# A gated attention-and-MLP kernel: full-array products next to P.V issued as four column strips, memory state as diagonal blocks

## Chip, core and metric

The kernel runs on one core of a Trainium2 chip. The metric is the device time of one execution in microseconds (us). The core's engines run side by side, each through its own list of instructions in order: PE (TensorE, matrix products into PSUM), DVE (VectorE), ACT (ScalarE), POOL (GpSimd) and SP (SyncE, which here only issues DMAs). They wait for one another through semaphores.

## What is computed

One layer over 2048 tokens of width 448, in bf16. A gate per token mixes two branches: attention in four segments of 512 tokens, with a linear memory of the earlier segments, and an MLP that mixes along the tokens.

```python
g = _sigmoid((x * gate_w).sum(-1, keepdims=True))
# attention: H = 16 heads of 28, N = 4 segments of L = 512
for s in range(N):
    p = _softmax(q_s k_s^T * 28**-0.5 + causal mask)
    a_dot = p @ v_s
    num = einsum('bhld,bhde->bhle', phi(q_s), M)
    den = einsum('bhld,bhd->bhl', phi(q_s), z)[..., None] + 1e-06
    o = gh * (num / den) + (1.0 - gh) * a_dot          # gh = sigmoid(beta), per head
    M = M + einsum('bhld,bhle->bhde', phi(k_s), v_s)
    z = z + einsum('bhld->bhd', phi(k_s))
a = o @ wo
# MLP over the token axis, F = 1792
u = gelu(einsum('bsd,sf->bdf', layernorm(x), w1) + b1)
b = einsum('bdf,fs->bds', u, w2) + b2
out = g * a + (1 - g) * b
```

(Indices are shortened; phi(t) is t + 1 above zero and exp(t) below.)

## The kernel before

Everything stays in on-chip memory between input and output. The work is cut into some 600 PE steps with names, and as many on the other engines:

- **Projections** `k0..k3`, `q0..q3`, `v..` (line 679): two products of 64 rows each run side by side on the two halves of the array's rows.
- **Scores** `scP_F` (938): for a pair P of attention units and one of five fills F, four heads at once on four strips of 28 rows. A unit is one segment and one group of four heads; there are 16 units. ACT takes the exponential (947) and POOL sets the masked triangle to zero (950).
- **P.V** `pvU` (975): for unit U, sixteen matmuls, four heads at once on four strips of 32 columns, with moving operands of 512, 384, 256 and 128 columns. The loop over `hl` puts head `hl` into PSUM partitions 32*hl to 32*hl+31. DVE transposes the result (`ta`, 991).
- **Memory** `mstS` (824): after each of three segments, phi(k)^T v as 16 full-array products of 128 by 128, four head groups over four token tiles. All 16 head-to-head blocks of a group are computed. DVE adds them up (`msta`, 837 and 840) and multiplies by `maskg`, which is zero outside the four diagonal blocks (`mstc`, 842). `memU` (961) is one product of 512 columns with that state, and `tm` (989) its transpose on DVE.
- **Output projection** `woT` (1026): four full-array products of 448 columns. `ag` (1032, 1036) takes it out of PSUM on ACT or DVE.
- **MLP** `uF-S` (1046), 14 x 16 products of 448 columns with the full array, and `yT-F` (1075), 16 x 14 of them, the last tile in two parts of 320 and 128 columns. GELU is five steps on ACT and DVE (1050 to 1063), and the output is made on DVE (`fin`, 1080).
- **Transposes of x** for the first 512 tokens, `trx0_0` and `trx0_1` (648): eight of 128 by 128 each, into two banks, then two copies out, `xTcp`, the even one on DVE and the odd one on ACT.

Every PE step has a mode, which the text keeps using: `f` for the full array, `h` for half the rows, `r` for the row strips of scores, `c` for the column strips of P.V.

The order of the steps is written out by hand, as a list of names per engine (`ORDER`); `u0-0:3=6` means the three steps from `u0-0` on, into PSUM bank 6. `Sched.plan` follows these lists and makes each step wait for what it reads and for the step that last used its bank. Banks 4 to 7 are handed round among all these steps; banks 0 to 3 belong to scores after the start. For some steps the list also says which of two engines does them.

Of the kernel before, what the change touches and what calls it, by code (L numbers as in the profile page):

```python
# [5 lines left out]
ACT = mybir.ActivationFunctionType  # L6
ALU = mybir.AluOpType
# [23 lines left out]
NFILL = 6  # L31

# [11 lines left out]
class Op:  # L44
    __slots__ = ("eng", "evspace", "fn", "deps", "order", "is_event", "ev_val", "knowledge", "waits", "name", "idx",
                 "cost", "lat", "prio", "mode", "start", "end", "pos", "nbytes", "alts", "rel", "port", "take",
                 "free")
# [26 lines left out]
class Sched:  # L74
# [13 lines left out]
    def op(self, eng, fn, reads=(), writes=(), name=None, dma=False, out=False, cost=100.0, prio=0.0, mode=None,  # L88
           nbytes=0, rel=0.0, port=False, take=None, use=(), alt=None):
# [14 lines left out]
        o.free = use  # L104
        for g in use:
            g.left += 1
# [45 lines left out]
    def plan(self, order):  # L152
# [7 lines left out]
        for e, text in order.items():  # L160
            seq[e] = []
            for tok in text.split():
                tok, _, banks = tok.partition("=")
                name, _, run = tok.partition(":")
                if run:
                    base, _, k = name.partition("-")
                    got = [byname["%s-%d" % (base, int(k) + i)] for i in range(int(run))]
                else:
                    got = [byname[name]]
                for o in got:  # L170
                    o.eng = e
                for g, b in zip(got[0].take, banks):
                    g.bank = int(b)
                seq[e] += got
        assert sum(len(v) for v in seq.values()) == len(self.ops)
# [28 lines left out]
        self.ops = line  # L204

# [48 lines left out]

def pe_cost(*cols):
    return sum(max(c, 64) / 2.4 + 2.0 for c in cols)
# [10 lines left out]
def pool_cost(n):  # L267
# [7 lines left out]
        warm fill0 fill1 fill2 fill3 fill4 trx0_0=45 fill5 gtr trx0_1=67 v03s v03a v03b v03c v03d k0a=45 k0b=67 k0c  # L275
        k0d q0a q0b q0d q0c v67a=46 sc0_0 k1a=57 v67c k1c sc0_1 k1b=64 k1d sc0_2 q1a=75 q1b=64 sc0_3 q1c q1d pv0=7
        sc0_4 u2-0:2=6 u1-0=5 u2-2:2 u0-0:3=4 u1-1 u2-4 u1-2:3 sc1_0 u2-5 u0-3 u1-5 u0-4 btr=7 u0-5 u1-6 u2-6 u0-6
        u2-7 u0-7:2 u1-7 u0-9 u4-0=7 u1-8:2 u0-10 sc1_1 u0-11 u1-10:3 u2-8:2 u1-13:3 u0-12 u2-10:2 u0-13 u2-12 u0-14
        u2-13 u0-15 u4-1 u2-14 u3-0=5 sc1_2 u4-2 u3-1:2 u4-3 u3-3 u4-4 u3-4 u2-15 pv1=4 sc1_3 u4-5 u3-5:2 u5-0:2=4
        u3-7 u5-2:2 u4-6:2 u5-4 u3-8 sc1_4 u4-8 u3-9 u5-5 u3-10:2 u4-9 u5-6 u3-12 u4-10 u3-13 u5-7 u3-14:2 u5-8:2  # L280
        u6-0=6 u4-11 u5-10 u4-12 sc2_0 u4-13 u5-11:2 u7-0=5 u4-14 u6-1 u7-1 u4-15 u7-2 u5-13 u6-2 u7-3 u6-3 u5-14
        sc2_1 u7-4:2 mst0=7 u7-6 u5-15 u7-7:3 u6-4:2 u7-10 sc2_2 pv3=7 pv2=4 u6-6:2 u8-0:3=7 u6-8:2 u7-11 u6-10 sc2_3
        u8-3 u7-12 u6-11 u7-13:3 u6-12:2 u9-0:2=4 u8-4 u6-14:2 u8-5 sc2_4 u8-6 u9-2 u8-7:2 u9-3 u8-9 u9-4 mem4=5
        u9-5:3 sc3_0 u8-10 u9-8 u8-11:2 u9-9:3 u8-13:3 u9-12:4 pv4=6 sc3_1 k2a=57 k2b=46 k2c k2d sc3_2 q2a=75 q2b=46
        q2c q2d sc3_3 v96a=57 v96b=46 v96c v96d sc3_4 pv6=7 pv5=5 u10-0:4=4 u11-0=6 u10-4 mem5=7 u10-5 mem6=5 u10-6
        u11-1 sc4_0 u13-0=7 u10-7 u13-1:2 u10-8:6 u11-2:3 sc4_1 u10-14 u13-3 u11-5 u13-4 u10-15 u11-6 u12-0=5 u11-7
        u12-1 u11-8 u13-5 u11-9:3 u12-2 u11-12:2 u13-6 sc4_2 u12-3:2 u11-14 u13-7 u12-5 mst1=4 u13-8 u11-15 u13-9
        u12-6 sc4_3 u12-7 u13-10 u12-8:2 u13-11:2 mem7=6 u12-10 u13-13 wo1=4 u12-11 sc4_4 pv7=6 wo0~2=4 u12-12
        u13-14:2 u12-13:3 wo3=6 wo2=4 sc5_0 k3a=67 k3b=54 k3c k3d sc5_1 v14a=67 pv8=5 v14c sc5_2 pv9=5 wo5=4 mem9=6
        q3a=75 q3b=46 q3c q3d sc5_3 mem8=5 y1-0:3=7 y0-0=4 y1-3 y3-0=6 y1-4:2 y0-1:2 y1-6 y0-3:2 y3-1 y1-7 y3-2:3 y1-8  # L290
        sc5_4 y1-9 y3-5 y0-5:2 y1-10 y0-7 wo4=5 y1-11 sc6_0 y0-8:2 y3-6 y0-10:2 y3-7 y1-12 y0-12:2 y3-8 y1-13 sc6_1
        y3-9:2 y4-0:2=5 y3-11 y4-2:2 y3-12 y4-4 y3-13 mem11=7 wo6=4 sc6_2 y4-5 mst2=7 pv11=6 pv10=4 sc6_3 y4-6 mem10=7
        y2-0=6 y4-7:2 y2-1 y6-0=4 y4-9 y2-2 y6-1 y4-10 sc6_4 y5-0=7 y6-2 y2-3:2 y4-11 y5-1 y2-5 y5-2 y6-3 y5-3 y6-4
        sc7_0 y2-6:2 y5-4 y4-12 y2-8 y5-5 y2-9 y5-6 y6-5 y4-13 y2-10 y5-7 sc7_1 y2-11 y5-8:2 y6-6 y2-12 mem12=5 y2-13
        y5-10 y6-7 y5-11:2 sc7_2 y6-8:4 y5-13 wo7=6 pv12=5 sc7_3 y6-12 mem13=7 y7-0:3=6 wo8=5 y7-3 y6-13 wo10=7 y7-4
        pv13=5 sc7_4 y7-5 wo9=4 y7-6:2 y8-0=7 y7-8 y9-0:2=5 y7-9:2 y9-2 mem14=4 y7-11 y8-1 y7-12 y9-3 y8-2 y9-4 y8-3:2
        y7-13 wo11=4 y8-5 y9-5 pv15=6 pv14=4 y9-6 y8-6 y9-7 mem15=6 y8-7:2 y9-8 y10-0=4 y9-9 y8-9:2 y10-1 y8-11 y9-10
        y10-2:2 y9-11 y11-0=6 y10-4:2 y11-1 y8-12 y10-6 y9-12 y11-2 y9-13 y8-13 y10-7:2 y11-3:7 y10-9 y11-10 y10-10
        y11-11 y10-11 y11-12 y10-12:2 y11-13 wo12=5 wo13=7 wo14=6 wo15=4 y12-0=5 y13-0:2=7 y12-1 y15-0=6 y12-2 y15-1
        y14-0:2=4 y13-2:2 y14-2 y13-4 y14-3 y12-3 y15-2 y14-4 y15-3 y13-5 y14-5:2 y13-6 y14-7 y12-4 y15-4 y13-7 y12-5  # L300
        y13-8 y14-8 y15-5 y14-9 y13-9:2 y15-6 y14-10 y15-7:2 y14-11 y13-11 y14-12 y15-9:2 y13-12 y15-11 y13-13
        y15-12:2 y12-6:2 y14-13 y12-8:6 y15-0~2=7 y15-1~2 y15-2~2 y15-3~2 y15-4~2 y15-5~2 y15-6~2 y15-7~2 y15-8~2
        y15-9~2 y15-10~2 y15-11~2 y15-12~2 y15-13~2
    """,
    "ACT": """
        ldx1 ldgwb ldgw xTcp0_01 xTcp0_11 cpv2 cpv0 cpv3 gt1 gt0 cpk0_0 gt3 gt2 ek0_0 cpk0_2 cpk0_3 cpk0_1 cpq0_3
        cpq0_2 cpq0_1 gt4 ek0_1 exp0_0=2 cpv6 gt7 gt6 exp0_1=3 cpk1_2 exp0_2=4 exp0_3=0 cpq1_2 tb cpv5 gt5 exp0_4=1
        ek0_2 eq1_1 exp1_0=5 exp1_1=6 gsq1 eq1_0 eq1_2 gsq0 exp1_2=2 ek0_3 gth0 exp1_3=3 gsq2 gth1 exp1_4=0 gth2 gsq3
        ek1_0 ek1_1 exp2_0=1 gsq4 gth3 exp2_1=4 gsq5 gth4 gvh5 eq1_3 exp2_2=0 gth5 ek1_3 exp2_3=3 gsq7 gsq6 exp2_4=2
        gth7 gth6 exp3_0=5 gsq8 gsq9 gvh9 ek1_2 exp3_1=6 cpk2_1 cpk2_3 cpq2_3 exp3_2=1 cpq2_1 cpv8 gt8 exp3_3=4 cpv10  # L310
        gt10 gt9 ek2_0 eq2_1 gt11 gt12 exp3_4=7 ek2_1 gth9 gth8 exp4_0=5 exp4_1=6 eq2_0 gsq10 gvh10 exp4_2=0 gsq11
        gvh11 exp4_3=2 gth10 ag1 gth11 exp4_4=3 gsq13 gsq12 gvh13 gvh12 ek2_2 exp5_0=1 cpk3_0 exp5_1=4 cpq3_3 cpv14
        cpv15 gt14 gt15 gth13 gth12 ag5 exp5_2=7 ek2_3 cpq3_0 cpq3_2 gt13 eq3_1 exp5_3=5 eq2_3 eq3_0 eq2_2 exp5_4=6
        exp6_0=0 exp6_1=2 ag6 exp6_2=3 eq3_2 exp6_3=5 exp6_4=6 exp7_0=1 exp7_1=4 exp7_2=7 ag7 exp7_3=0 ag8 ag10 ag9
        exp7_4=2 eq3_3 ag11 ag12 ag15
    """,
    "DVE": """
        bns0 bna0 bns1 xTcp0_00 gw bns2 xTcp0_10 padk0 bns3 bna1 padq0 bna3 padq2 bna2 cpv1 padq3 ln0 ln2 ob0 mk0_0
        phk0_0 gcol0 ln3 bns4 cpv4 cpq0_0 bns5 bns7 bna4 bns6 bns9 bna5 cpv7 mk0_1 cpk1_1 ln1 bns13 cpk1_0 bna6 cpk1_3
        bna7 cpq1_3 bna13 bns8 bns11 bns15 bna9 bns10 cpq1_0 bna10 bna11 ln6 bna8 cpq1_1 bna15 bns14 ln4 ln9 bns12 ln5  # L320
        ln7 bna14 omgh ta0 ln8 gh ln10 bna12 oc0 b1c mo0 ln11 b2c oc1 ln13 mk0_2 b1h ln12 ln14 mg0 b1s mq1_1 ln15 oc2
        mo1 oc3 phk0_1 gvh1 phk0_2 gvh0 gcol1 garg0 phq1_1 mg1 garg1 ta1 mo2 mk0_3 omg1 gelu0 omg0 phk0_3 gvh2 rec1
        garg2 mg2 gelu1 rec0 gvh3 gelu2 garg3 oa1 mk1_0 mo3 phk1_0 gvh4 mg3 mk1_1 garg4 gelu3 phk1_1 msta0 oa0 ta3
        gelu4 garg5 mstc0 ot0 ta2 mq1_0 gelu5 mk1_3 phq1_0 rec3 gvh7 gvh6 rec2 garg7 mq1_2 garg6 tm4 phq1_2 gelu6 oa2
        gelu7 gvh8 ta4 eps4 phk1_3 b2g1 mq1_3 mk1_2 phk1_2 rec4 cpk2_0 cpk2_2 ot1 ot2 oa4 garg8 cpq2_0 cpq2_2 oa3 om4
        garg9 cpv9 cpv12 cpv11 mk2_0 ta6 ta5 mq2_1 tm5 eps5 tm6 phk2_0 eps6 mk2_1 rec5 rec6 om6 gelu8 phq2_1 gelu9
        phk2_1 ot3 oa5 phq1_3 gcol2 om5 garg10 ot4 ot5 msta1 garg11 mstc1 tm7 b2g0 eps7 mq2_0 gelu10 oa6 gelu11 ta7
        ag0 ot6 ag3 ag2 rec7 garg12 om7 oa7 cpk3_1 cpk3_2 cpk3_3 garg13 ta8 ot7 ta9 tm9 gelu13 gelu12 phq2_0 cpq3_1
        cpv13 mk2_3 mk2_2 phk2_2 eps9 phk2_3 rec9 tm8 omg2 om9 mq2_2 eps8 oa9 phq2_2 mq2_3 rec8 phq2_3 om8 ag4 fin1
        fin0 mq3_0 tm11 fin3 eps11 oa8 phq3_0 msta2 ta11 ta10 tm10 rec11 eps10 mstc2 rec10 ot8 mq3_1 oa11 om10 phq3_1  # L330
# [26 lines left out]
def build_kernel(nc, X, WQ, WK, WV, WO, BETA, W1, B1, W2, B2, GW, OUT):  # L357
# [459 lines left out]
    def do_mst(s):  # L817
# [15 lines left out]
        def mps():  # L833
            return bank(b)[:, 0:512].rearrange("p (g c) -> p g c", g=NHG)
# [378 lines left out]
```

## Time and profile before

| | us |
|---|---|
| median of 6 runs | 176.99 |
| lowest and highest run | 176.29, 178.24 |
| the profiled execution | 176.33 |
| span of its instructions | 174.6 |

| engine | busy us | share | instructions |
|---|---|---|---|
| DVE | 145.6 | 83% | 321 |
| ACT | 128.0 | 73% | 154 |
| POOL | 70.5 | 40% | 101 |

The span is from the first to the last instruction of the program; 1.73 us of the execution lie around it. The granted PE clock is full in all 40 slices. Busy time of PE counts an instruction from its start to its modelled end, and instructions overlap, so the distance from one start to the next is what is read here.

### The profile page before, as it was taken

The page shows a single profiled execution, that of the slowest core. Times are in us where ns is not written, and L with a number is a line of the kernel's source. Part 1 is how long each engine was busy: PE and PEld are TensorE (multiplying, and loading weights), DVE is VectorE, ACT ScalarE, POOL GpSimd, SP SyncE. Part 2 cuts the span into 40 slices and gives each one's busy share as a digit, 9 for nine tenths or more (in the row PEclk, how much of TensorE's full clock was granted, in tenths as well). Part 3 has the DMA queues.
Part 4 walks back from the last instruction along what each step waited for, and adds up shares of the span by engine and source line. Part 5 has one row for each costly group of instructions (what it writes and reads, how often), then busy time and mean ns, then how long its engine had stood idle before and what let it go on. Part 6 is the DMA issues. An engine that isn't in the chain of part 4 may idle for free.

```text
span 174.6 us, 3705 instructions
## 1 busy us (share of the span) xinstructions
PE 168.6 (97%) x1435; PEld 80.2 (46%) x1435; DVE 145.6 (83%) x321; ACT 128.0 (73%) x154; POOL 70.5 (40%) x101
## 2 busy tenths in 40 slices
PE   8999989998999999999999999999999999999994
PEld 4444324443455444444454434444544444555552
DVE  1579999799899999999989998978996988996014
ACT  2269989599999999999889989987878756101100
POOL 7240186332925303662061783029627945050000
PEclk9999999999999999999999999999999999999999
DMA  5999989219982593391047950033420890918003
GB/s 145 300 216 354 242 150 255 71 36 260 129 239 52 84 278 91 78 236 48 0 102 220 289 137 1 4 71 116 133 59 0 226 297 6 256 41 257 30 0 105
DMA packets 49745, 24.51 MB, mean 140 GB/s; under 512 B 14256, under 2 KB 49488, under 8 KB 49728
## 3 DMA queue, kind: packets, MB, share of 16 engines
q1 hardware_dynamic: 49576, 24.16, 55.2%
q8 instruction: 11, 0.18, 0.4%
q10 hardware_dynamic: 152, 0.12, 0.2%
q14 instruction: 6, 0.05, 0.2%
HBM read 18.76 MB, written 2.36 MB: 121 GB/s over the span
## 4 chain that ended last, share of the span: by engine, by line
PE 78%; DVE 10%; ACT 5%; DMA 2%; SPq 2%; issue 1%; POOL 1%
PE t L1075 25%; PE t L1046 22%; PE t L679 10%; PE t L1026 7%; PE t L938 6%; PE t L975 5%; DMA t<-in_A_wk_dram 2%; ACT t L947 2%; DVE t L881 2%; PE t L824 2%; PE t L961 1%; DVE t L774 1%; DVE t L1058 1%; POOL t L1006 1%; ACT t L798 1%
## 5 line engine op out<-in xcount | busy, mean ns | idle before, releaser
L947 ACT ACTIVATE t<-t 128x2048 bf16<-128x2048 f32 x40 | 75.1, 1877 | 9.0 <-PE t L938 8.6
L950 POOL TENSOR_SCALAR_AFFINE_SELECT t<-t 128x512 bf16<-128x512 bf16 x64 | 43.9, 704 | 50.8 <-ACT t L947 50.1
L1046 PE MATMUL t<-t 128*128 128x448 bf16 x224 | 47.0, 353 | 0.5 <-DVE t L991 0.5
L1075 PE MATMUL t<-t 128*128 128x448 bf16 (+2 forms) x238 | 46.4, 342 | 0.0
L679 PE MATMUL t<-t 64*128 64x512 bf16 (+1 forms) x308 | 35.3, 367 | 1.6 <-DVE t L881 0.4
L1075 PEld LDWEIGHTS t<-t 128*128 128x128 bf16 x238 | 22.0, 98 | 20.7 <-issue 2.5
L1046 PEld LDWEIGHTS t<-t 128*128 128x128 bf16 x224 | 20.2, 98 | 21.4 <-issue 3.9
L1006 POOL TENSOR_TENSOR t<-t 128x448 bf16<-128x448 f32 x12 | 15.5, 1298 | 27.3 <-DVE t L1004 16.0
L679 PEld LDWEIGHTS t<-t 64*128 64x128 bf16 x308 | 15.4, 94 | 18.6 <-PE t L679 1.3
L1080 DVE SCALAR_TENSOR_TENSOR t<-t 128x448 bf16<-128x448 f32 (+2 forms) x17 | 10.7, 650 | 11.3 <-PE t L1075 11.0
L1032 ACT ACTIVATE t<-t 128x448 bf16<-128x448 f32 x10 | 7.2, 724 | 16.2 <-PE t L1026 16.2
L938 PE MATMUL t<-t 28*128 28x512 bf16 (+3 forms) x256 | 15.8, 301 | 0.1
L1026 PE MATMUL t<-t 128*128 128x448 bf16 x64 | 14.1, 353 | 0.0
L881 DVE BATCH_NORM_STATS2 t<-t 128x6 f32<-128x448 bf16 x16 | 9.4, 608 | 3.5 <-DMA t<-in_A_x_dram 3.5
L991 DVE STREAM_TRANSPOSE t<-t 128x512 f32<-128x512 f32 x16 | 11.1, 705 | 1.0 <-PE t L975 0.9
L1012 DVE STREAM_TRANSPOSE t<-t 128x512 bf16<-128x512 bf16 x16 | 11.0, 695 | 0.6 <-POOL t L1006 0.6
L975 PE MATMUL t<-t 128*32 128x512 bf16 (+3 forms) x256 | 10.9, 301 | 0.5 <-DVE t L883 0.4
L938 PEld LDWEIGHTS t<-t 28*128 28x128 bf16 x256 | 4.5, 92 | 14.0 <-ACT t L947 6.3
L989 DVE STREAM_TRANSPOSE t<-t 128x512 f32<-128x512 f32 x12 | 8.5, 706 | 1.8 <-PE t L961 1.8
L1050 ACT ACTIVATE t<-t 128x448 f32<-128x448 f32 x14 | 8.8, 635 | 1.0 <-PE t L1046 0.6
L1058 DVE SCALAR_TENSOR_TENSOR t<-t 128x448 f32<-128x448 f32 x14 | 9.1, 650 | 0.5 <-ACT t L1053 0.4
L1063 DVE SCALAR_TENSOR_TENSOR t<-t 128x448 bf16<-128x448 f32 x14 | 8.8, 638 | 0.0
(77 smaller groups left out, 183.7 us busy)
## 6 DMA issues: line engine op xcount, KB each, us to landing
t<-in_B_w_dram SPq DMA_DIRECT2D x7, 1024.0 KB, 6.5
t<-in_B_w_dram SPq DMA_DIRECT2D x8, 896.0 KB, 5.9
out_dram<-t SPq DMA_DIRECT2D x15, 112.0 KB, 1.8
t<-in_A_x_dram SPq DMA_DIRECT2D x3, 448.0 KB, 5.0
t<-in_A_wo_dram SPq DMA_DIRECT2D x4, 98.0 KB
t<-in_A_wk_dram SPq DMA_DIRECT2D x1, 336.0 KB, 4.2
t<-in_A_wq_dram SPq DMA_DIRECT2D x1, 336.0 KB, 4.1
spare_heads<-t SPq DMA_DIRECT2D x8, 32.0 KB
```

What stands on the lines that cost most here:

```text
L679: last = e.matmul(bank(o["b"])[:, 0 : o["n"]], o["w"](r, c), o["x"](r, c), start=first, stop=end, skip_group_check=True)
L881: op("DVE", lambda e: e.bn_stats(st6[:, t, :], xh[:, t, :]), reads=[R_x[t]], writes=[R_st6[t]], name=f"bns{t}", cost=512, prio=P_PROJ - 10)
L938: last = e.matmul(bank(hl)[:, c0 : c0 + w], kT[r, hg, s * 512 + j * 128 : s * 512 + j * 128 + 128], qT[r, hg, s * 512 + 128 * j : s * 512 ...
L947: op("ACT", lambda e: e.activation(pslot(g), ps[:, 0:4, :], ACT.Exp, scale=SCALE), reads=R_bank[0:4], writes=[g.res], take=g, name=f"exp{p ...
L950: op("POOL", lambda e, c0=c0: e.affine_select(pslot(g)[:, :, c0 : c0 + 128], pslot(g)[:, :, c0 : c0 + 128], pattern=[[0, 4], [1, 128]], co ...
L975: last = e.matmul(bank(cb)[32 * hl : 32 * hl + 32, 128 * j : 512], vaug[:, 4 * s + j, 32 * h : 32 * h + 32], pslot(P_fill[u // 2][f])[:, h ...
L991: dv(lambda e: e.transpose(t2[:, 0, :], bank(cb)[:, 0:512]), [bres(cb)], [R_tt[tb][0]], "ta", 630, use=(cb,))
L1006: op("POOL", lambda e: e.tensor_tensor(o3, n3[0], n3[1], op=ALU.add), reads=R_tt[tb], writes=[R_ob[tb]], name=f"o{u}", cost=1280, port=Tru ...
L1012: dv(lambda e: e.transpose(oT[:, hg, s * 512 : s * 512 + 512], o), [R_ob[tb]], qres(hg, s), "ot", 635)
L1026: last = e.matmul(bank(b)[:, 0:D], oT[:, hg, T * 128 : T * 128 + 128], wo_sb[:, hg, :], start=(hg == 0), stop=(hg == NHG - 1), skip_group_ ...
L1046: op("PE", lambda e, st=st: e.matmul(bank(b)[:, 0:D], w1c[:, st, f2 * 128 : f2 * 128 + 128], xh[:, st, :], start=(st == 0), stop=(st == NT ...
L1075: op("PE", lambda e, ft=ft: e.matmul(bank(b)[:, 0 : c1 - c0], w2c[:, ft, t2_ * 128 : t2_ * 128 + 128], uT[:, ft, c0:c1], start=(ft == 0), ...
```

## The change

There are four parts.

1. A new pass, `Sched.columns`, runs over the PE list. Between two scores or projections (modes `r` and `h`) it looks at the stretches of `f` steps next to a `c` step. Where such a stretch has at most 30 steps (60 between two `c` steps), and all of its steps can be split, each step's product is issued as four matmuls of 32 output columns.

```diff
+NEAR = 30
+    def columns(self, seq):
+        k = 0
+        while k < len(seq):
+            n = k
+            while n < len(seq) and seq[n].mode in "fc":
+                n += 1
+            part = [-1] + [i for i in range(k, n) if seq[i].mode == "c"] + [-1]
+            for a, b in zip(part, part[1:]):
+                if a < 0 and b < 0:
+                    continue
+                gap = seq[k if a < 0 else a + 1 : n if b < 0 else b]
+                limit = NEAR if a < 0 or b < 0 else 2 * NEAR
+                if len(gap) <= limit and all(o.split is not None for o in gap):
+                    for o in gap:
+                        o.alts = {"PE": (o.split,) + o.alts["PE"][1:]}
+            k = n + 1
...
+def mm(e, out, w, x, split, **kw):
+    if not split:
+        return e.matmul(out, w, x, skip_group_check=True, **kw)
+    for q in range(0, 128, 32):
+        last = e.matmul(out[q : q + 32], w[:, q : q + 32], x, skip_group_check=True, **kw)
+    return last
```

`u`, `y`, `wo` and `mem` can be split; transposes and warm-up products cannot.

2. The memory state is computed as its diagonal blocks only: 64 matmuls of 32 output columns by 32 moving columns take the place of 16 of 128 by 128, and the step's mode is `c`. `msta` then handles 128 elements per partition instead of 512, and `mstc` spreads them over the four blocks while it masks.

```diff
                 for hg in range(NHG):
-                    last = e.matmul(bank(b)[:, hg * 128 : hg * 128 + 128],
-                                    phk[:, 4 * s + jj, hg * 128 : hg * 128 + 128],
-                                    vaug[:, 4 * s + jj, hg * 128 : hg * 128 + 128], ...
+                    for hl in range(4):
+                        c = slice(hg * 128 + 32 * hl, hg * 128 + 32 * hl + 32)
+                        last = e.matmul(bank(b)[32 * hl : 32 * hl + 32, hg * 32 : hg * 32 + 32], phk[:, 4 * s + jj, c],
+                                        vaug[:, 4 * s + jj, c], ...
...
-        op("DVE", lambda e: e.tensor_tensor(mst_sb[:, s, :, :], mst_f32[:], maskg[:], op=ALU.mult),
+        op("DVE", lambda e: e.tensor_tensor(mst_sb[:, s, :, :].rearrange("p g (b c) -> p g b c", c=32),
+                                            mst_f32[:, :, None, :].to_broadcast([128, NHG, 4, 32]),
+                                            maskg[:].rearrange("p g (b c) -> p g b c", c=32), op=ALU.mult),
```

3. The transposes of x become four steps, one per bank, `trx0_0`, `trx0_1`, `trx1_0`, `trx1_1`, and each copy can be done by ACT or DVE. In the new list ACT does three and DVE one (`xTcp0_11`).

4. All five lists are written anew. The steps are the same, but the order of PE, the banks, the order of the DMAs and the choice of ACT or DVE for some twenty steps differ; `padk1` and `padx0` go from POOL to DVE. The head of the PE list, before and after:

```diff
-        warm fill0 fill1 fill2 fill3 fill4 trx0_0=45 fill5 gtr trx0_1=67 v03s v03a v03b v03c v03d k0a=45 k0b=67 k0c
-        k0d q0a q0b q0d q0c v67a=46 sc0_0 ...
+        warm fill0 fill1 fill2 fill3 fill4 trx0_1=4 trx0_0=5 trx1_1=6 fill5 gtr trx1_0=7 v03s v03a v03b v03c k0a=45
+        v03d k0c k0b=67 q0a k0d q0b q0d q0c v67a=45 sc0_0 ...
```

and a stretch with the first split steps, around `pv1`:

```diff
-        ... pv1=4 sc1_3 u4-5 u3-5:2 u5-0:2=4 u3-7 ...
+        ... sc1_2 u2-9:3 pv1=6 u2-12 u3-9:2 u5-0:2=7 u2-13 sc1_3 u3-11 u2-14 u4-0=6 ...
```

## The prediction

> **What bounds the kernel now.** I read the page's busy rows and chain first, then the waits, then the order of time on PE.
>
> ```profile
> PE 168.6 (97%) x1435; PEld 80.2 (46%) x1435; DVE 145.6 (83%) x321; ACT 128.0 (73%) x154; POOL 70.5 (40%) x101
> PE 78%; DVE 10%; ACT 5%; DMA 2%; SPq 2%; issue 1%; POOL 1%
> PE t L1046 <- DVE t L991: 0.5, 1, 0.5
> 50.00:70.00 20.00, 20.00 (x194) 9.44 (x194) 19.57 (x43) 19.61 (x24) 6.55 (x8) 1.00 0.63 142
> ```
>
> The first two rows are the page's (busy time, chain that ended last), the third is from the waits, the fourth is one stretch of 20 us: PE, PEld, DVE, ACT, POOL, each with its count, then clock and DMA. PE carries the chain, and after 110 us it hardly ever stops. But in 50 to 70 us DVE and ACT are full as well (19.57 and 19.61 of 20): there a faster PE may only wait for them.
>
> PE's busy time overlaps itself, so I take distances between starts from the timeline:
>
> ```profile
> 54.57 1.27 PE L975 MATMUL t<-t 128*32 128x512 bf16 x32
> 55.77 1.92 PE L1046 MATMUL t<-t 128*128 128x448 bf16 x9
> 57.63 0.39 PE L938 MATMUL t<-t 28*128 28x512 bf16 x4
> 57.95 2.82 PE L1046 MATMUL t<-t 128*128 128x448 bf16 x14
> 60.71 0.40 PE L938 MATMUL t<-t 28*128 28x384 bf16 x8
> 61.04 1.50 PE L1046 MATMUL t<-t 128*128 128x448 bf16 x7
> 62.37 0.38 PE L961 MATMUL t<-t 128*128 128x512 bf16 x1
> ```
>
> (Start, duration, engine, line, shape, count.) Seven products of 448 columns before a `mem`, also full array, take 62.37 - 61.04 = 1.33 us, 190 ns each; over the trace's 465 such pairs of starts the median is 189. Fourteen before a row-strip step take 60.71 - 57.95 = 2.76 us, and 14 x 189 is only 2.65: about 0.1 us more. So **a change of mode costs some 95 ns**. Start to start, f to f is 189 but f to r 285 and f to c 283; from a 128-column strip back to f it is 152 against 56 within f. All differ by 94 to 96.
>
> With 96 changes of mode in the list before, the span divides so: 155.0 us of streaming, 9.1 of mode changes (96 x 95 ns), 6.8 of PE waiting (1.4 of it warm-up matmuls at a slower pace in the first 4 us), 0.8 before the first matmul and 2.6 after the last one's start. The waits that count are 0.48, 0.57 and six of 0.16 to 0.48 up to 25.4 us, 0.29 around the transpose of the biases at 30.6 (`btr`, line 855), 0.68 at 41.2, 0.26 at 71.4 and 0.36 at 107.2.
>
> **Mode changes.** I went through the new PE list with the rule of `columns`: 71 steps are split (55 `u`, 7 `y`, 3 `mem`, 6 `wo` of four products), that is 89 products and 3 x 89 = 267 more matmuls. Counting again, the list has 86 changes instead of 96; unsplit, with `mst` on strips, it would have 108. Changes between f and c fall from 12 to 1, those at scores and projections remain. **Saved: 10 x 95 ns = 0.95 us**, all on PE's path. It can't be more, since a change is a fixed piece of each count; it is less by what a split product costs above 189 ns.
>
> **A split product.** The nearest row is P.V itself: four strips start within 11 ns, and the next four start 215 ns after the first for 512 columns, 162 for 384, 108 for 256. That is columns / 2.4 + 2 ns, as the full array has it, so 448 columns give 189: **no loss**. The whole pair of P.V units above says the same: 54.57 to 55.77 is 1.20 us for 2 x 1280 columns (1.07 us), eight groups' 2 ns and one mode change.
>
> Two rules of the Trainium skill speak against it. "TensorEngine Tiling (Array Packing)", Restrictions, says that column tiling switches off the fast weight load. Here four 32-column loads start within some 12 ns, each about 96 ns long in the record, against 98 ns for one 128-column load, and four more follow within a 56 ns group; if they went one behind the other at the rate of "TensorE: Matmul & The Clock Gate", LDWEIGHTS (columns / 1.2, so 27 ns), they would need 107, still below 189. The second page's section "Wait — 56ns, not 53.3ns?" gives 62 ns of sequencer time per matmul where it isn't decoded in hardware: 4 x 62 = 248 ns, 59 more than 189, and 89 x 59 = 5.2 us lost. The trace is against that: in the P.V pair at 54.57 the semaphore wait ahead of the second unit is met 0.40 us after the first unit's first load, so its 32 instructions had passed in 0.40 us, at most 13 ns each. Eight instructions per split product are then 104 ns of 189. By the row the cost is 0, by the rule +5.2 us; I take the row, since it is this kernel's PE.
>
> **The memory state.** Before, 16 x 56 ns = 0.89 us per segment, three times (line 824). After, 64 strip pairs. In P.V the smallest group of four, 128 columns, takes 55 ns, of which 53 are streaming; a group of 32 columns has no row. Low end: starts 4 ns apart, 16 groups x 16 ns = 0.26 us. High end: 128 instructions at 13 ns = 1.66 us. The same page's floor of 25 ns between starts would make it 64 x 25 = 1.6 us, but the trace starts different strips 4 ns apart. I take **no change** (16 x 56, the nearest row); ends -1.9 and +2.3 us for three. On DVE `msta` handles a quarter: 684 ns for 512 elements, about 150 for the smallest copies, so some 0.28 for 128, 0.4 us saved three times. `mstc` has as many elements as before.
>
> **Start.** The four transposes per bank are the same 16. `xTcp0_01` can begin after four instead of eight, 0.22 us earlier, but `xTcp0_00` now follows it on ACT (0.54 further). Both are done at about 5.5 us, and `v03s` began at 5.73, after a wait for its weights' DMA: hidden, with 0.2 to spare. Before, `k0a` waited 0.57 us and began at 9.14, when POOL had finished its pads (8.01 to 8.99). With `padk1` and `padx0` on DVE ahead of `padk0` (0.2 + 0.57 us after the landing at 7.98), it can begin 0.35 earlier; but `v03d` (0.7 us of PE work that filled the time) now stands behind it, which loses 0.35. I take 0, +-0.35. `bns3` moves into idle DVE time, `ob0` to the front.
>
> **Waits that go.** At 41.2 us PE stood 0.68 because `u5-0` took `pv1`'s bank 4 and `ta1` had not emptied it: between them lay `sc1_3` and three `u`. In the new list `u5-0` takes bank 7, and `pv1`'s bank 6 is next wanted by `u4-0`, six `u`, `sc1_3` and two `u` later: about 2.0 us against 1.0. `ldb1` is issued before `ldw1_2` instead of behind it and two gathers; but `btr` is also wanted about 3 us earlier, just when it should land (issued at 26.5 before, 3 us earlier now, some 4 us to land), so its 0.29 is not counted. New banks make new waits: `mst0` now takes bank 6 behind `pv2`, with `u7-10`, `sc2_2` and three `u` between (1.2 us), and `ta2` needs 0.2 + 0.7 on a full DVE. The gaps of the list are otherwise like before: last step of scores to `pv15` is 4.1 us, which `exp7_4` (1.88) and two masks (0.70 each) just fill. The choice of engines moves about 0.75 us of work to DVE, the smaller `msta` take 1.2 away. I count **-0.3 us** for all waits together, half of what the 0.68 would give.
>
> DMA: the same transfers, with `ldw1_0` ahead of `ldw1_1` because `u0` comes first now. SP stood 5.9 us at `ldbeta` behind the first weight chunk; it will stand as long at `ldw1_1` instead, with `tk0_0` queued behind either way. The last 132 full products keep their kind, so the tail is as before.
>
> **Sum**, against the profiled execution: 176.33 - 0.95 + 0 + 0 - 0.3 = 175.1. The median shown lies 0.66 above that execution: 176.99 - 1.25 = **175.7 us**.
>
> **Rivals.** 0.5% of this kernel is 0.9 us, about what can be told from no change.
>
> - *Forecast* (0.45): mode changes saved, strips free. 175.7, own range 174.8 to 176.5.
> - *More* (0.17): the waits at 41.2 and 30.6 both go and `mst` halves (-0.45 x 3): 176.99 - 0.95 - 0.97 - 1.35 = 173.7. For it: DVE gains 0.45 us net. Against it: an `mst` group has 8 instructions to issue.
> - *The gain is waited away* (0.15): in 42 to 71 us PE had no wait of note, with DVE and ACT at 98%; the new list must fit as well. 0.95 saved, as much lost: 176.9.
> - *Bank waits take over, slower* (0.16): `pv1`'s kind of wait comes back at `mst0`, `pv3`, `mst1` and `wo9`, each one DVE step late (0.65 us): 176.99 - 0.95 + 4 x 0.65 = 178.6. It decides from two such waits on, as 1.5 x 0.65 is the saving. For it: DVE 19.57 of 20, and `ta2` stands behind four GELU and output steps of about 0.65. Against it: the list leaves 1.2 us or more at each.
> - *Strips cost their issue, slower* (0.07): 62 ns per matmul, 176.99 - 0.95 + 5.2 = 181.2. It decides from 0.95 us / 89 = 11 ns per split product. Against it: P.V's 2 ns. That the split doesn't happen, leaving 108 changes (+1.1 us), is excluded by the lists: they meet the rule.
>
> Faster: 0.36 of the forecast's 0.45, 0.17, and 0.02 of the third, so 0.55. Slower: 0.16, 0.07, 0.01, so 0.24. The rest, 0.21, is the same. The range 173.2 to 178.7 leaves out the issue case and the ends of the others.
>
> **What would show it.** Matmuls near 1435 + 267 + 144 = 1846. Strip products of 448 columns beginning every 189 ns, and the c-to-r distance of 96 ns over streaming at their ends. `mst` from first to last start near 0.9 us. No PE wait for line 991 at about 41 us. Wrong would be: strip groups at 200 ns or more; PE waits for DVE's transposes between 42 and 71 us; `k0a` no earlier than 9.1.

## The result and the profile after

The changed kernel takes 175.25 us (median of 19 runs) where the kernel before took 176.7 (38 runs beside it): a ratio of 0.9918, with a 95% interval of 0.9899 to 0.9937. The forecast was 175.7, faster. The profiled execution went from 176.33 to 175.21 us, its span from 174.6 to 173.5.

The page's busy rows and chain after the change, then a row of the waits, then the stretch of 50 to 70 us:

```profile
PE 166.7 (96%) x1846; PEld 80.7 (47%) x1846; DVE 145.2 (84%) x323; ACT 128.1 (74%) x154; POOL 69.7 (40%) x99
PE 70%; DVE 17%; ACT 5%; DMA 2%; issue 2%; SPq 2%; ACTq 0%
PE t L278 <- issue: 1.3, 1, 1.3
50.00:70.00 20.00, 18.60 (x314) 9.07 (x314) 18.66 (x41) 18.16 (x21) 5.89 (x8) 1.00 0.81 127
```

The 1846 matmuls are those counted from the lists. The row that matters is the third. "issue" is idle time for which the profile shows no reason, and PE has 1.3 us of it in one piece. The stretch that PE filled before (20.00 of 20) now has 18.60, and DVE and ACT are no longer full.

The timeline of PE around that piece, in the changed kernel (start, duration, line, shape, count; line 280 is a split product, 852 the memory state, 1005 P.V, 967 scores, 278 a whole product):

```profile
51.01 1.70 PE L280 MATMUL t<-t 128*32 128x448 bf16 x32
52.73 0.73 PE L1005 MATMUL t<-t 128*32 128x512 bf16 x16
53.27 0.38 PE L280 MATMUL t<-t 128*32 128x448 bf16 x4
53.58 0.40 PE L967 MATMUL t<-t 28*128 28x256 bf16 x8
53.91 0.75 PE L280 MATMUL t<-t 128*32 128x448 bf16 x12
54.49 0.67 PE L852 MATMUL t<-t 128*32 128x32 bf16 x64
54.98 0.57 PE L280 MATMUL t<-t 128*32 128x448 bf16 x8
55.36 0.73 PE L1005 MATMUL t<-t 128*32 128x512 bf16 x16
56.19 0.40 PE L967 MATMUL t<-t 28*128 28x512 bf16 x4
56.52 1.88 PE L278 MATMUL t<-t 128*128 128x448 bf16 x9
59.67 0.54 PE L278 MATMUL t<-t 128*128 128x448 bf16 x2 [1.28 <-issue]
```

Three things can be read off. Eight strip matmuls from 54.98 to 55.36 are two split products in 0.38 us, 190 ns each: a split product costs what a whole one does. The memory state runs from 54.49 to 54.98, **0.49 us, where it took 0.89**. And PE stands still between the ninth product after 56.52 (`u6-14`, which starts at 58.04) and the next one (`u6-15`, at 59.67), in the middle of a run of equal products. `u6-15` waits for no semaphore, and the load of its weights had begun at 58.04. By the list no datum of it can be late either: `u7-15`, two steps before, had read the same rows of x, and `u6-14` the same chunk of weights and the same bank.

### Where the time went

Start distances, step by step, divide the two profiled executions like this:

| us | before | after | difference |
|---|---|---|---|
| streaming, without the memory state | 151.42 | 151.42 | 0 |
| memory state, three times | 2.67 | 1.47 | -1.20 |
| mode changes, 95 ns each | 9.12 (96) | 8.17 (86) | -0.95 |
| all waits and overheads | 7.91 | 8.97 | +1.06 |
| first start to last start | 171.13 | 170.03 | -1.10 |

In the last group the wait for `pv1`'s bank fell from 0.68 to 0.27 (now at `u4-0`) and 0.37 went at `q3b`. `k0a`'s wait fell from 0.58 to 0.22 while `v03s` rose from 0.48 to 0.94. Split products took 0.23 more than streaming, a wait of 0.20 for a bank that DVE empties came at `pv2`, and one of 0.19 for ACT's exponential in front of the scores behind `pv3`. The rest are smaller pieces. One outweighs them all: **1.44 us between `u6-14` and `u6-15`**, the stall above (1.63 from start to start, less 0.19).

### What the stall is: a late page of instructions

PE's program reaches it by DMA too. The page's DMA section has a queue for it (packets, MB, share of time), before and after:

```profile
q8 instruction: 11, 0.18, 0.4%
```

```profile
q8 instruction: 14, 0.23, 0.6%
```

The packets on this queue are 16,384 bytes each. The change adds 821 matmuls, weight loads and waits to PE's list (2942 to 3763 records) and three packets, some 270 records a packet. So PE reads its list in pages; below they are taken as 256 instructions, the figure of the Trainium skill's page that is named at the end. In the record of single packets the fetch that matters begins at 57.20 us and ends at 58.32, and PE runs again at 59.67. The 256 PE records before the stall had been used up in 4.8 us, from 53.2 to 58.0, since `mst0` alone has 128 and each split product 8. Before the change, any 256 PE records in a row took 10.3 us or more.

### The profile page after: what moved, and what is told of

Its sections match the earlier page's. It is cut to its first block, busy times and chain, and to the rows that moved or that the text cites. A ratio compares the mean times of both kernels' runs of the same rounds, so it can differ in the third digit from the quotient of the medians.

```text
span 173.5 us, 4532 instructions
## 1 busy us (share of the span) xinstructions
PE 166.7 (96%) x1846; PEld 80.7 (47%) x1846; DVE 145.2 (84%) x323; ACT 128.1 (74%) x154; POOL 69.7 (40%) x99
## 4 chain that ended last, share of the span: by engine, by line
PE 70%; DVE 17%; ACT 5%; DMA 2%; issue 2%; SPq 2%; ACTq 0%
PE t L278 41%; PE t L705 13%; PE t L280 6%; PE t L967 5%; PE t L1005 4%; DVE t L1089 3%; DMA t<-in_A_wk_dram 2%; DVE t L1087 2%; ACT t L976 2%; DVE t L1094 2%; ACT t L1081 2%; DVE t L1040 2%; DVE t L910 1%; DVE t L789 1%; DVE t L755 1%
## 5 line engine op out<-in xcount | busy, mean ns | idle before, releaser
L278 PE MATMUL t<-t 128*128 128x448 bf16 (+1 forms) x449 | 86.7, 348 | 1.4 <-issue 1.3
L979 POOL TENSOR_SCALAR_AFFINE_SELECT t<-t 128x512 bf16<-128x512 bf16 x64 | 44.4, 718 | 54.9 <-ACT t L976 54.4
L278 PEld LDWEIGHTS t<-t 128*128 128x128 bf16 x449 | 41.5, 98 | 41.9 <-issue 6.5
L280 PE MATMUL t<-t 128*32 128x448 bf16 (+1 forms) x356 | 20.2, 354 | 0.0
L1005 PE MATMUL t<-t 128*32 128x512 bf16 (+3 forms) x256 | 11.4, 300 | 0.5 <-DVE t L893 0.5
L280 PEld LDWEIGHTS t<-t 128*32 128x32 bf16 x356 | 8.5, 96 | 6.3 <-issue 1.8
L1087 DVE TENSOR_SCALAR t<-t 128x448 f32<-128x448 f32 x10 | 6.6, 668 | 3.5 <-ACT t L1081 3.5
L1005 PEld LDWEIGHTS t<-t 128*32 128x32 bf16 x256 | 6.6, 96 | 6.1 <-POOL t L979 1.5
```

Source lines behind the costliest of these rows:

```text
L278: return e.matmul(out, w, x, skip_group_check=True, **kw)
L280: last = e.matmul(out[q : q + 32], w[:, q : q + 32], x, skip_group_check=True, **kw)
L979: op("POOL", lambda e, c0=c0: e.affine_select(pslot(g)[:, :, c0 : c0 + 128], pslot(g)[:, :, c0 : c0 + 128], pattern=[[0, 4], [1, 128]], co ...
L1005: last = e.matmul(bank(cb)[32 * hl : 32 * hl + 32, 128 * j : 512], vaug[:, 4 * s + j, 32 * h : 32 * h + 32], pslot(P_fill[u // 2][f])[:, h ...
```

## Experiments

Theory A is that late page, theory B that the stall belongs to the step (a bank or a datum that comes late).

**Moving the page ends.** Two kernels, with NOPs behind the products of `u0` to `u3`, three or one each:

```diff
-                return mm(e, bank(b)[:, 0:D], w1c[...], xh[:, st, :], split, ...)
+                last = mm(e, bank(b)[:, 0:D], w1c[...], xh[:, st, :], split, ...)
+                for _ in range(3 if ft < 4 else 0):      # 1 in the second kernel
+                    e.nop(nofuse=True)
+                return last
```

> The changed kernel with 192 empty instructions (NOPs) put into PE's list, three behind each of u0 to u3, nothing else. Theory A (the 1.44 us stall of PE at 58.0 us is a late instruction page: mst0's 128 instructions and the strips use up one 256-instruction page in 4.8 us, and the next isn't there): the pages now end elsewhere, the page with mst0 lasts about 10 us by the trace's start times, the stall is gone: 175.25 - 1.44 = 173.8 us. Theory B (the stall belongs to that step of the list, a bank or a datum that comes late): it stays at u6-14, 175.2 us or, by the NOPs' own issue, more.

> The changed kernel with 64 NOPs, one behind each of u0 to u3. Theory A: the pages end 64 instructions earlier; by the start times the page around mst0 then lasts 3.6 us instead of 5.0, and the one around mst1 3.7 instead of 6.5, so the first stall grows by some 1.4 us and a second one of 1 to 2.5 us comes at about 85 us: 177 to 179 us, slower than the changed kernel and than before. Theory B: 175.2 us as without NOPs.

Measured: 174.68 us, ratio 0.9898 (0.9871 to 0.9924), and 175.56, ratio 0.9932 (0.9904 to 0.996). But the traces show that **the NOPs never reached the chip**: both have the same 3763 PE records and 14 instruction packets as the changed kernel. So neither tests what it was written for; they are 14 more runs of the changed kernel, two of them profiled, in the same set as the two experiments below. Their median is 174.83 us, where the kernel before has 176.37 in that set (25 runs). That the two medians differ by 0.9 us shows how far the time of one program can move. As profiles they tell something else. The stall in the first, from the timeline of PE:

```profile
56.69 1.68 PE L278 MATMUL t<-t 128*128 128x448 bf16 x8
58.63 0.92 PE L278 MATMUL t<-t 128*128 128x448 bf16 x4 [0.27 <-issue]
```

and in the second:

```profile
56.67 1.88 PE L278 MATMUL t<-t 128*128 128x448 bf16 x9
60.09 0.92 PE L278 MATMUL t<-t 128*128 128x448 bf16 x4 [1.54 <-issue]
```

It is at the same instruction in all three (one record falls on the other side of the merge in the first), but of three lengths, and each length follows the fetch:

| execution | fetch begins | ends | PE resumes | after the end | stall | span |
|---|---|---|---|---|---|---|
| changed kernel | 57.20 | 58.32 | 59.67 | 1.35 | 1.44 | 173.5 |
| with three NOPs | 56.03 | 57.18 | 58.63 | 1.45 | 0.43 | 172.8 |
| with one NOP | 57.44 | 58.55 | 60.09 | 1.54 | 1.70 | 174.2 |

Between the first execution and the second the fetch moved by 1.2 us, the resumption by 1.0 and the span by 0.7; between the second and the third by 1.4, 1.5 and 1.4. Theory B has nothing that moves like this. What decides when the fetch begins is not shown. The trace points at the data DMAs: the new order issues a chunk of weights at 52.0 us (before the change at 46.9 and 59.2), and from 54 to 57 us the packets of the 16 DMA engines add up to 1.12 of their time (packets overlap in the record), where it was 0.36 before. PE had entered the page before at about 53.2, and the fetch began at 57.20. That it stood behind these transfers fits, but no run tests it. The eight runs of the second kernel lie in two groups, 174.5 to 174.7 and 175.5 to 176.0 us; a page that comes early or late would do that, but only one of them has a profile.

**No split.** Whether mode changes have the price that the prediction gave them:

```diff
-NEAR = 30
+NEAR = -1
```

> The changed kernel with no product split (NEAR = -1), strips for the memory state kept: 108 mode changes instead of 86. Prediction's price of 95 ns per change: +2.1 us; the split products' 0.4 us over streaming goes; with theory A the stall at 58 us goes too (534 fewer instructions, pages elsewhere): 175.25 + 2.1 - 0.4 - 1.44 = 175.5 us. With theory B for the stall: 176.9 us. Rival (mode changes are hidden behind DVE and ACT in the full stretch, strips gain nothing): 175.2 or less with the stall still there.

Measured: 175.8 us, ratio 0.997 (0.995 to 0.9989), against 0.9918 with the split. These two intervals don't meet, though that of the second kernel above (0.9904 to 0.996) overlaps a little; against the 174.83 us of the 14 runs beside it the split is worth 1.0 us, half a per cent. The price shows in its trace too: 108 changes, and 10 of the 12 from the full array to strips cost 93 or 94 ns over streaming. The time is 0.3 us above the sum with theory A and 1.1 below the one with theory B, and there is no stall at 58 us: 534 instructions fewer, 12 packets instead of 14. Not all agrees: 2.09 us more of mode changes, less 1.44 and some 0.2 of the split products' own cost, would have added 0.4 us to the span, and it grew by 1.5 (175.0). The rest are other waits, the largest in this row of the waits:

```profile
PE t L278 <- DMA t<-in_B_w_dram: 0.6, 1, 0.6
```

That is `y6-0` at 128.6 us, whose weights landed late in this execution (0.73 from start to start); ahead of the first scores PE stands 0.69 where it was 0.22. The profiled run, at 176.72, was the slowest of its twelve, so the median is the better measure here.

**The memory state as full blocks.** `do_mst` as before the change, all else kept:

```diff
-                    for hl in range(4):
-                        c = slice(hg * 128 + 32 * hl, hg * 128 + 32 * hl + 32)
-                        last = e.matmul(bank(b)[32 * hl : 32 * hl + 32, hg * 32 : hg * 32 + 32], phk[:, 4 * s + jj, c], ...
+                    last = e.matmul(bank(b)[:, hg * 128 : hg * 128 + 128],
+                                    phk[:, 4 * s + jj, hg * 128 : hg * 128 + 128], ...
```

> The changed kernel with the memory state as full 128 by 128 blocks as before (16 products each, msta on 512 elements), splits kept where the rule still meets: 88 mode changes, 58 split steps. The strips' gain of 0.40 us per segment measured in the changed kernel's trace (0.49 against 0.89) is lost: +1.2, two more changes +0.2; with theory A the stall at 58 us goes because 96 instructions fewer are issued at mst0: -1.44, sum 175.2 us. Theory B: 176.6 us. If msta's smaller size on DVE matters in the full stretch 50 to 70 us, up to 0.8 us more than either.

Measured: 176.44 us, ratio 0.9991 (0.9972 to 1.0009), no gain over the kernel before. That is the time which theory B gave, and yet the trace has no stall at 58 us. A new one stands where PE needed a bank (timeline of PE; line 705 is a projection, 1084 the GELU step that empties the bank of a `u`):

```profile
66.72 0.40 PE L964 MATMUL t<-t 28*128 28x384 bf16 x8
68.06 1.25 PE L705 MATMUL t<-t 64*128 64x512 bf16 x10 [0.94 <-DVE t L1084]
```

DVE ended that step at 67.91 and PE went on at 68.06. So the page's 1.44 us went and 1.01 of waiting for DVE came, and 0.46 at `mst1` (for the DMA transposes of phi(k)). The time alone would have told the wrong story.

The wait for DVE doesn't come merely because PE is no longer held up by its page. In the execution with three NOPs, where the stall was only 0.43 us, PE reached the same projection at 66.93 and did not wait: DVE had ended the GELU step at 66.72, 1.2 us earlier than here. Three DVE pieces of this trace make up that difference: `msta0` takes 0.69 us instead of 0.29, `mstc0` 1.12 instead of 0.68, and two GELU steps together 1.59 instead of 1.16. The first is the change's own saving on DVE; why the other two are longer is not shown. So DVE did matter in this stretch, as the last sentence of the expectation allowed for.

Without the memory strips the kernel loses 0.7%, without the split 0.5%, and the whole change brings 0.8%. These are not shares of the gain: each removal brings new waits with it.

Not tried: the old lists with split and strips alone, a shift of the pages by real instructions, and a version without the stall. The share of the new lists in the gain stays open, and so does what such a version would win.

## Why the prediction was right, and where not

- **The price of a mode change held.** 96 to 86 changes at 95 ns gave -0.95; f to r is still 285 ns in the new trace, and a split product to scores 296 to 308 in four cases. The lowest is 189 + 96 and the 11 ns by which the fourth strip starts after the first. Changes between f and c were 11 in the trace before, not 12, and are 1; the totals of 96 and 86 are right. Without the split the kernel is 0.5% slower.
- **A split product is free, as the P.V row had said.** Between split products the median distance is 189 ns (68 pairs, 188 to 200). The 5.2 us that the rule of 62 ns per matmul would have cost did not come, and the loads of the strips stayed hidden; whether the fast weight load was off is not shown. All 89 products together cost 0.23 us over streaming, mostly the 11 ns of skew at the ends of runs. The P.V row had that too: ten of its sixteen groups of 512 columns take 226 or 227 ns before the change, not the 215 that the prediction read.
- **The memory state was mis-sized.** The term was 0, with ends of -1.9 and +2.3; measured -1.20. Sixteen groups of four strips take 0.49 us, 31 ns per group, where the prediction took the 56 of a 128-column group as the nearest row. Its high end rested on 13 ns per instruction, which was a bound from above and not a price: here 128 instructions ran in 490 ns, under 4 each. This row of the groups shows the DVE part, one `msta` (mean 274 ns):

```profile
L867 DVE TENSOR_TENSOR t<-t 128x128 f32<-128x128 f32 x2 | 0.5, 274 | 0.6 <-PE t L852 0.6
```

  The estimate from two rows had been 0.28 us.
- **The waits went the other way**: +1.06 instead of -0.3. The bank wait at 41 us fell by 0.4 to 0.27, where none was to be left. Of the bank waits of the slower rival one of 0.2 us came, at `pv2`. What the prediction didn't have was the page of instructions. It asked whether instructions *issue* fast enough, and not whether they *arrive* fast enough: 534 + 288 more instructions (matmuls and loads of the splits and of the memory state) were priced at 0 because the engine could take them.
- **Start**: the sum was 0 and came out +0.1 (`k0a` 0.36 less, `v03s` 0.46 more): the first scores begin at 16.54 us instead of 16.45. `k0a` began at 8.67 us instead of 9.14, where 0.35 earlier was told. These two waits vary: in the three executions of this program `v03s` waits 0.94, 0.25 and 0.16 us and `k0a` 0.22, 0.23 and 0.58, and the first scores begin 0.04 to 0.25 later than before.

So the median fell by 1.45 where 1.25 was forecast, through two errors of over a microsecond that nearly cancelled: 1.20 us of memory state not counted, and 1.44 of stall not seen. The price of the mode changes and of the strips was understood; that the total came so close was luck.

## What to carry to other kernels

Four strips of 32 columns in place of a full-array product of 448 columns cost no array time here (189 ns either way), so products that stand between strip work can join its mode; count the mode changes and price them from the distances between starts. But count the instructions too: here 256 of them passed in 4.8 us, and PE outran the fetch of its own program. Such a stall shows as "issue" in the middle of equal steps, and its length differs from one execution to the next. When an experiment removes a wait and the time doesn't fall, look in its trace for the wait that took its place before giving up the theory.

## What the runs showed of the hardware

PE's instructions come in packets of 16 KB, some 270 records of the trace each, and PE went on 1.35 to 1.54 us after the transfer of the one it waited for had ended (three executions). The Trainium skill, "Runtime: NRT & Kernel Launch", section "Instruction fetch mechanics", has the 16 KiB blocks of 256 instructions, and says that the fetch hides behind the issue of the instructions; here it didn't, with a block used up in 4.8 us, and PE stood for 0.43, 1.44 and 1.70 us. Strips of 32 by 32 columns ran at 31 ns per group of four, 7.7 ns per matmul with its weight load, over 64 in a row.
